# The product of probabilities and v as one float32 product of 64 stationary columns in every batch of a fused attention and MoE kernel

## The chip, the cores and the metric

The kernel runs on one core of one Trainium2 chip, as one program. The metric is the device time of one execution in microseconds (us); lower is better. The core has TensorE (PE; its weight loads are shown as PEld), VectorE (DVE), ScalarE (ACT), GpSimd (POOL) and SyncE (SP), whose queue issues the DMAs here.

## The reference

Three stages follow one another, all in float32: block-causal attention over 4 batches of 8 heads (576 positions, head size 64, blocks of 64), a dense layer with the maximum of three products, and a layer of 4 experts. The change touches the last line of the attention alone.

```python
scores = scale * np.matmul(q, k.transpose(0, 1, 3, 2))     # (4, 8, 576, 64) each
scores = np.where(mask, scores, -1000000000.0)              # block_i >= block_j, blocks of 64
attn = np.exp(scores - np.max(scores, axis=-1, keepdims=True))
attn = attn / (np.sum(attn, axis=-1, keepdims=True) + 1e-09)
attn_out = np.matmul(attn, v)                               # the product of this change
...
h = np.maximum(np.maximum(x @ w1, x @ w2), x @ w3)          # first layer, 2304 tokens
x = h @ w_out
...
out += p[:, e:e + 1] * (np.maximum(x @ w1[e], 0.0) @ w2[e]) # second layer, 4 experts
```

## The kernel before

**Stages.** Heads are numbered g = 0 to 31, eight to a batch, two to a pair. Batch 0 of the attention runs by itself (up to some 103 us). From then on the attention of batch b is mixed with the first layer of batch b - 1: a `Filler` object puts products of `moe1` (the tiles `m`, line 509) between the steps of a head, up to a due count worked out from the head number. The first layer of batch 3 follows alone from 476 us, then the second layer to the end. During batch 1 the weights of the first layer are also converted and split (class `Convert`, lines 432 to 457, on ACT, DVE and POOL) and stored for the later batches.

**Order.** The code issues its steps in a list per head: transposes of probabilities (`ta`, `tb`), scores of the head after next (`s0`, `s1`), values (`va`, `vb`). A scheduler of the framework then orders the instructions of each engine before the program runs; on the chip each engine works its list off in that order.

**Steps of a head that matter here.** `scores` (line 249, tile `st`) makes the scores, DVE finds the extremes (line 263, `mn`), ACT the exponentials (line 270, `p`), POOL multiplies by the reciprocal sums (line 281). `turn_probs` transposes the probabilities by 128 x 128 pieces (line 313, tile `tt` in PSUM) and copies them to SBUF in banks of at most 512 columns. `values` multiplies them with v into the PSUM tiles `pv`, and the result goes to `xf` in SBUF.

**Two ways of that product.** In batch 0 (`g < H`, `values32`) the transposed probabilities stay float32 (`eh`) and v is the raw tile `vraw`, 64 columns as stationary operand: 10 products per head of 128, 384, 384, 128, 256 and five times 64 moving columns, into the lower half of the PSUM partitions; each float32 product becomes two instructions on PE. One ACT copy per part brings the result to `xf` (line 352). In batches 1 to 3 both operands are split into a rounded high part and the rest, as float32r: ACT makes `eh` (line 318) and DVE makes `el` (line 319); POOL makes `vs`, whose 128 columns hold the high part of v beside the low part (lines 161 to 167). The same 10 products are then made twice, with `eh` and with `el` (lines 365 and 373), each one instruction of 128 stationary columns. The two halves of the PSUM partitions are added by an ACT copy to `tmp` and a DVE addition to `xf` (lines 384 and 385).

**Buffers.** `eh` and `el` have one buffer for each part; `pv` comes from its own two PSUM banks in batch 0 and from the four banks shared with `st`, `tt` and `tq` later on.

Of the kernel before, what the change touches and what calls it, by code (L numbers as in the profile page):

```python
# [6 lines left out]
F32 = mybir.dt.float32  # L7
F32R = mybir.dt.float32r
# [17 lines left out]
def program(tc, q, k, v, w1, w2, w3, w_out, probs, e_w1, e_w2, out):  # L26
# [14 lines left out]
    def f(ap):  # L41
        return ap.bitcast(F32)
# [82 lines left out]
    def prep_pair(g):  # L125


        vraw = pairs[g]["vraw"]
        if g < NPAIR and g % 2:

            spare = mp.tile([P, 2 * QW + 2 * S], F32R, name="spare", tag="hh")
            q1, q2 = spare[:, 0:QW], spare[:, QW:2 * QW]
            kk = spare[:, 2 * QW:].rearrange("x (h s) -> x h s", h=2)
        else:
            q1, q2 = (ap_.tile([P, QW], F32R, name=x, tag=x, bufs=1)[:] for x in ("q1", "q2"))
            kk = ap_.tile([P, 2, S], F32R, name="kk", tag="kk", bufs=1)[:]
        nc.gpsimd.memset(q1[:, QT + 64:QT + 128].bitcast(U32), 0)
        q_main = q1[:, 0:QT].rearrange("x (h r p) -> x r h p", h=2, p=64)
        q_tail = q1[:, QT:QW].rearrange("x (t p) -> x t p", p=64)[:, 0:3:2].unsqueeze(1)
        k_all = kk.rearrange("x h (r p) -> x r h p", r=R)  # L140

        def to(n, a, z, step=1):

            if n:
                return k_all[:, a:z:step]
            return q_tail if a == R - 1 else q_main[:, a:z:step]

        turn = turn_parts if g < SPLIT else turn_raw
        turn(g, to, 0)
        if g == 0:  # L150
            nc.scalar.copy(q2[lo], q1[hi])
            nc.vector.tensor_copy(q2[hi], q1[lo])
        else:
            nc.sync.dma_start(out=f(q2[lo]), in_=f(q1[hi]))
            nc.sync.dma_start(out=f(q2[hi]), in_=f(q1[lo]))
        yield
        turn(g, to, 1)
        pairs[g].update(q1=q1, q2=q2, kk=kk)
        if g < NPAIR:
            return  # L160
        vs = ap_.tile([P, 2, 5, P], F32R, name="vs", tag="vs", bufs=2)
        nc.gpsimd.memset(vs[lo, :, 4, :].bitcast(U32), 0)
        for pp, js in ((both, slice(0, 4)), (hi, slice(4, 5))):
            vh = vs[pp, :, js, 0:64]
            rounded(nc.gpsimd, vh, vraw[pp, :, js])
            nc.gpsimd.tensor_tensor(vs[pp, :, js, 64:128], vraw[pp, :, js], f(vh), op=ALU.subtract)
        pairs[g]["vs"] = vs

    def turn_parts(g, to, half):

# [127 lines left out]
    def turn_probs(g, part):  # L298

        hd = heads[g]  # L300
        banks = PARTS[part]
        w = (1024, 256, 640)[part]
        eh = ap_.tile([P, w], F32 if g < H else F32R, name="eh", tag=f"eh{part}", bufs=1)
        el = None if g < H else ap_.tile([P, w], F32R, name="el", tag=f"el{part}", bufs=1)
        (pairs[g // 2] if part == 2 else hd)["e", part] = (eh, el)
        pt = hd["p"] + [pairs[g // 2]["p4"]]
        for n in banks:
            o = 512 * (n - banks[0])
            tt = ps_x.tile([P, 512], F32, name="tt", tag="x")
            c = 0  # L310
            for j, i in BANKS[n]:
                k0 = S - P if j == 4 else j * P
                nc.tensor.transpose(tt[:, c:c + P], pt[i][:, k0:k0 + P], ident)  # L313
                c += P
            if g < H:
                (nc.scalar.copy if n else nc.vector.tensor_copy)(eh[:, o:o + c], tt[:, 0:c])
                continue
            nc.scalar.copy(eh[:, o:o + c], tt[:, 0:c])
            nc.vector.tensor_tensor(el[:, o:o + c], tt[:, 0:c], f(eh[:, o:o + c]), op=ALU.subtract)
        if part == 1 and g % 2 == 0:  # L320
            turn_probs(g, 2)

# [8 lines left out]
            todo += [(j, slice(384, 448), 2, slice(j * P + h * 64, j * P + h * 64 + 64)) for j in range(5)]  # L331
        return todo

    def values32(g, part):

        hd, vraw, h = heads[g], pairs[g // 2]["vraw"], g % 2
        if part == 0:
            hd["pv"] = [ps_v.tile([P, 512], F32, name=f"pv{i}", tag="v") for i in range(2)]
            et = hd["e", 0][0]
            nc.tensor.matmul(out=hd["pv"][0][lo, 0:P], lhsT=vraw[:, h, 0], rhs=et[:, 0:P], start=True, stop=True)  # L340
        for n, (j, to, which, of) in enumerate(products(g, part)):
            et = (pairs[g // 2] if which == 2 else hd)["e", which][0]
            rows = hi if j == 4 else both
            nc.tensor.matmul(  # L344
                out=hd["pv"][1][lo, to], lhsT=vraw[rows, h, j], rhs=et[rows, of],
                start=part == 0 and n == 0, stop=j == 4,
            )
        if part == 0 and h == 0:
            pairs[g // 2]["xf"] = mp.tile([P, S], F32, name="xf", tag="xf", bufs=4)
        xf = pairs[g // 2]["xf"]  # L350
        qs = (slice(0, P), slice(P, S))[part]
        nc.scalar.copy(xf[lo if h == 0 else hi, qs], hd["pv"][part][lo, 0:qs.stop - qs.start])
        if part:
            del heads[g]

    def values(g, part):
        if g < H:
            values32(g, part)
            return
        hd, vs, h = heads[g], pairs[g // 2]["vs"], g % 2  # L360
        if part == 0:

            hd["pv"] = [ps_x.tile([P, 512], F32, name=f"pv{i}", tag="x") for i in range(2)]
            for n, et in enumerate(hd["e", 0]):
                nc.tensor.matmul(
                    out=hd["pv"][0][:, 0:P], lhsT=vs[:, h, 0], rhs=et[:, 0:P], start=n == 0, stop=n == 1
                )
        pv = hd["pv"][1]
        todo = products(g, part)
        for n in range(2):  # L370
            for m, (j, to, which, of) in enumerate(todo):
                et = (pairs[g // 2] if which == 2 else hd)["e", which][n]
                nc.tensor.matmul(  # L373
                    out=pv[:, to], lhsT=vs[:, h, j], rhs=et[:, of],
                    start=part == 0 and n == 0 and m == 0, stop=part == 1 and n == 1 and j == 4,
                )
        if part == 0 and h == 0:
            pairs[g // 2]["xf"] = mp.tile([P, S], F32, name="xf", tag="xf", bufs=4)
        xf = pairs[g // 2]["xf"]
        own, other = (lo, hi) if h == 0 else (hi, lo)  # L380
        qs = (slice(0, P), slice(P, S))[part]
        src = hd["pv"][part][:, 0:qs.stop - qs.start]
        tmp = ap_.tile([P, S - P], F32, name="tmp", tag="tmp", bufs=1)[own, 0:qs.stop - qs.start]
        nc.scalar.copy(tmp, src[other])
        nc.vector.tensor_tensor(xf[own, qs], src[own], tmp, op=ALU.add)
        if part == 0:
            return
        del heads[g]


    tiles = []
# [545 lines left out]
```

## Time and profile before

| | us |
|---|---|
| median of 3 runs | 1335.26 |
| lowest and highest run | 1331.67, 1337.66 |
| the profiled execution, device time | 1333.35 |
| its span, first to last instruction | 1331.6 |

| stretch of the profiled execution | us | PE busy | DVE busy | what runs |
|---|---|---|---|---|
| batch 0 | 0 to 103 | 87.30 | 69.05 | attention alone |
| batches 1 to 3 | 103 to 476 | 366.05 | 262.75 | attention, and first layer of the batch before |
| first layer of batch 3 | 476 to 600 | 115.93 | 57.10 | no attention |
| second layer | 600 to 1331 | 721.00 | 529.49 | experts |

Busy time of PE counts an instruction from its start to its modelled end, and those overlap, so a PE that is busy all the time is read by how many instructions start in a stretch, and by the time from the start of one row to the start of the next.

### The profile page before, as it was taken

How to read it: one execution, taken by the hardware profiler on the slowest of the kernel's cores; microseconds unless marked ns; L12 is line 12 of the kernel's file. 1: busy time of each engine (PE TensorE's matmuls, PEld its weight loads, DVE VectorE, ACT ScalarE, POOL GpSimd, SP SyncE). 2: the span in 40 equal slices, each digit the busy share in tenths (PEclk: the TensorE clock that was granted, in tenths of full speed). 3: DMA queues.
4: the chain of work that ended last, by engine and by line, in shares of the span. 5: the costliest groups of instructions: out<-in, count | busy, mean ns of one | idle time of the engine just before them, and what ended most of it. 6: DMA issues, size and time to landing. Idle time of an engine off the chain costs nothing.

```text
span 1331.6 us, 20943 instructions
## 1 busy us (share of the span) xinstructions
PE 1290.3 (97%) x7670; PEld 1189.9 (89%) x7670; DVE 918.4 (69%) x1685; ACT 542.0 (41%) x1219; POOL 628.7 (47%) x639
## 2 busy tenths in 40 slices
PE   7899989999999989989999999999999999999998
PEld 6569989999999989989999997999999889999997
DVE  6858999665656561178777679677777877777753
ACT  5666656544544430144333343333333433333330
POOL 4856777333334332265444456444454644444420
PEclk9889999999999989999999999999999999999999
DMA  8845677555433344232222222222222133222211
GB/s 200 223 114 137 211 222 213 162 153 145 140 120 117 111 154 147 86 96 88 64 64 79 64 64 87 88 64 64 64 72 78 50 114 91 71 64 64 64 32 48
DMA packets 146983, 142.86 MB, mean 107 GB/s; under 512 B 64576, under 2 KB 112704, under 8 KB 146880
## 3 DMA queue, kind: packets, MB, share of 16 engines
q1 hardware_dynamic: 146880, 141.52, 36.0%
q8 instruction: 60, 0.98, 0.3%
q14 instruction: 43, 0.35, 0.1%
HBM read 114.86 MB, written 17.30 MB: 99 GB/s over the span
## 4 chain that ended last, share of the span: by engine, by line
PE 85%; DVE 9%; issue 2%; DMA 1%; POOL 1%; ACT 1%; SPq 1%; ACTq 0%; POOLq 0%; DVEq 0%
PE m L793 24%; PE m L509 20%; PE o L855 9%; PE o L854 9%; PE o L853 9%; PE st L249 4%; PE pv L373 3%; PE tt L313 3%; PE pv L344 1%; PE tq L175 1%; DVE wt L456 1%; DVE t L715 1%; DVE hl L818 1%; PE tq L194 1%; DMA arena<-in_q 1%
## 5 line engine op out<-in xcount | busy, mean ns | idle before, releaser
L509 PE MATMUL m<-xh,wt 128*128 128x288 f32 x1152 | 259.5, 303 | 1.5 <-DVE mt L547 1.5
L853 PE MATMUL o<-w2h,hh 128*128 128x512 f32 x576 | 224.8, 391 | 4.9 <-DVE arena L860 4.9
L855 PE MATMUL o<-w2h,hl 128*128 128x512 f32 x576 | 225.1, 391 | 0.9 <-DVE hl L818 0.9
L854 PE MATMUL o<-w2l,hh 128*128 128x512 f32 x576 | 224.7, 390 | 0.0
L509 PEld LDWEIGHTS m<-xh,wt 128*128 128x128 f32 x1152 | 193.4, 190 | 2.8 <-DVE mt L547 2.1
L818 DVE SCALAR_TENSOR_TENSOR hl<-c,hh 128x384 fp32r<-128x384 f32 x144 | 166.9, 1179 | 34.1 <-ACT hh L817 33.8
L686 POOL TENSOR_TENSOR w2l<-r,w2h 128x512 fp32r<-128x512 f32 x96 | 130.3, 1378 | 88.1 <-ACT w2h L685 88.0
L509 PE MATMUL m<-xl,wt 128*128 128x288 f32 x576 | 171.5, 298 | 0.0
L686 POOL TENSOR_TENSOR sl<-s,sh 128x1024 fp32r<-128x1024 f32 x48 | 117.4, 2446 | 78.4 <-ACT sh L685 78.4
L686 POOL TENSOR_TENSOR al<-r,ah 128x512 fp32r<-128x512 f32 x48 | 64.4, 1342 | 175.0 <-ACT ah L685 172.0
L860 DVE SCALAR_TENSOR_TENSOR arena<-o,pr,arena 128x512 f32<-128x512 f32 x126 | 93.7, 744 | 71.4 <-PE o L855 71.4
L853 PEld LDWEIGHTS o<-w2h,hh 128*128 128x128 f32 x576 | 108.2, 188 | 23.6 <-DVE arena L860 6.0
L855 PEld LDWEIGHTS o<-w2h,hl 128*128 128x128 f32 x576 | 108.3, 188 | 22.1 <-DVE hl L818 1.6
L817 ACT ACTIVATE hh<-c 128x384 fp32r<-128x384 f32 x144 | 71.2, 519 | 133.2 <-DVE c L812 133.2
L854 PEld LDWEIGHTS o<-w2l,hh 128*128 128x128 f32 x576 | 108.5, 188 | 17.8
L281 POOL TENSOR_SCALAR p<-p,sm 128x128 f32<-128x128 f32 (+2 forms) x144 | 86.4, 617 | 55.1 <-ACT p L270 27.5
L509 PEld LDWEIGHTS m<-xl,wt 128*128 128x128 f32 x576 | 109.5, 190 | 0.6
L270 ACT ACTIVATE p<-st,mn 128x128 f32<-128x128 f32 (+3 forms) x144 | 78.7, 554 | 52.3 <-DVE mn L263 52.0
L685 ACT CAST ah<-r 128x512 fp32r<-128x512 f32 x48 | 29.8, 621 | 156.8 <-issue 117.8
L547 DVE TENSOR_TENSOR mt<-m,mt 128x288 f32<-128x288 f32 x96 | 43.6, 454 | 70.6 <-PE m L509 68.3
L509 PE MATMUL m<-hh,wo 128*128 128x288 f32 x384 | 84.5, 301 | 0.4 <-ACT arena L558 0.4
L549 POOL TENSOR_SCALAR hh<-mt 128x288 fp32r<-128x288 f32 x48 | 23.2, 483 | 125.9 <-DVE mt L547 120.7
(166 smaller groups left out, 3047.2 us busy)
## 6 DMA issues: line engine op xcount, KB each, us to landing
wt<-held SPq DMA_DIRECT2D x54, 512.0 KB, 4.0
r<-in_moe_w SPq DMA_DIRECT2D x48, 512.0 KB, 3.7
r<-in_moe_w SPq DMA_DIRECT2D x96, 256.0 KB, 2.6
arena<-in_moe_w SPq DMA_DIRECT2D x18, 512.0 KB, 4.8
held<-wt SPq DMA_DIRECT2D x18, 512.0 KB, 3.5
wo<-held SPq DMA_DIRECT2D x12, 768.0 KB, 4.3
q<-q SPq DMA_DIRECT2D x26, 304.0 KB, 4.3
arena<-in_q SPq DMA_DIRECT2D x32, 144.0 KB, 3.2
```

What stands on the lines that cost most here:

```text
L249: nc.tensor.matmul(out=st[:, o + c:o + c + n], lhsT=pair[part][:, q0:q0 + P], rhs=pair["kk"][:, x, c:c + n], start=m == 0, stop=m == len(t ...
L270: nc.scalar.activation(x, st[:, o:o + w], ACTF.Exp, bias=mn[:, col:col + 1], scale=-1.0, accum_out=sm[:, col:col + 1],)
L281: nc.gpsimd.tensor_scalar(x, x, sm[:, col:col + 1], 1.0, op0=ALU.mult, op1=ALU.mult)
L509: nc.tensor.matmul(out=out_, lhsT=w, rhs=x, start=m == 0, stop=m == n - 1)
L686: (low or nc.gpsimd).tensor_tensor(dst_l, raw, f(dst_h), op=ALU.subtract)
L793: nc.tensor.matmul(out=m, lhsT=w, rhs=x, start=start and n == 0, stop=stop and n == 3 * KH - 1, skip_group_check=True,)
L817: nc.scalar.activation(h, src, ACTF.Relu)
L818: nc.vector.scalar_tensor_tensor(l, src, 0.0, f(h), op0=ALU.max, op1=ALU.subtract)
L853: nc.tensor.matmul(out=o, lhsT=hh[:, ts], rhs=wh, start=i == 0, stop=False)
L854: nc.tensor.matmul(out=o, lhsT=hh[:, ts], rhs=wl, start=False, stop=False)
L855: nc.tensor.matmul(out=o, lhsT=hl[:, ts], rhs=wh, start=False, stop=i == G - 1)
L860: nc.vector.scalar_tensor_tensor(acc, ov, pr[:, tt, e:e + 1], acc, op0=ALU.mult, op1=ALU.add)
```

## The change

In batches 1 to 3 the product is made as in batch 0: v raw in float32, the transposed probabilities copied once as float32. The split of both operands goes: POOL's `vs` (memset, rounding, subtraction), DVE's `el`, and the second half of the products. So does the addition of the two halves: `xf` is one ACT copy again. The copy of the first bank of each head, which ACT made as `eh`, is now made by DVE (the line that batch 0 had). The tile of transposed probabilities is called `et` and has two buffers for each part in place of one `eh` and one `el`. `pv` stays in the shared PSUM banks from batch 1 on. Function `values32` becomes `values`, with a choice of the PSUM pool.

```diff
     def prep_pair(g):
...
-        if g < NPAIR:
-            return
-        vs = ap_.tile([P, 2, 5, P], F32R, name="vs", tag="vs", bufs=2)
-        nc.gpsimd.memset(vs[lo, :, 4, :].bitcast(U32), 0)
-        for pp, js in ((both, slice(0, 4)), (hi, slice(4, 5))):
-            vh = vs[pp, :, js, 0:64]
-            rounded(nc.gpsimd, vh, vraw[pp, :, js])
-            nc.gpsimd.tensor_tensor(vs[pp, :, js, 64:128], vraw[pp, :, js], f(vh), op=ALU.subtract)
-        pairs[g]["vs"] = vs
...
     def turn_probs(g, part):
...
-        eh = ap_.tile([P, w], F32 if g < H else F32R, name="eh", tag=f"eh{part}", bufs=1)
-        el = None if g < H else ap_.tile([P, w], F32R, name="el", tag=f"el{part}", bufs=1)
-        (pairs[g // 2] if part == 2 else hd)["e", part] = (eh, el)
+        et = ap_.tile([P, w], F32, name="et", tag=f"et{part}", bufs=2)
+        (pairs[g // 2] if part == 2 else hd)["e", part] = et
...
-            if g < H:
-                (nc.scalar.copy if n else nc.vector.tensor_copy)(eh[:, o:o + c], tt[:, 0:c])
-                continue
-            nc.scalar.copy(eh[:, o:o + c], tt[:, 0:c])
-            nc.vector.tensor_tensor(el[:, o:o + c], tt[:, 0:c], f(eh[:, o:o + c]), op=ALU.subtract)
+            (nc.scalar.copy if n else nc.vector.tensor_copy)(et[:, o:o + c], tt[:, 0:c])
...
-    def values32(g, part):
+    def values(g, part):
...
-            hd["pv"] = [ps_v.tile([P, 512], F32, name=f"pv{i}", tag="v") for i in range(2)]
-            et = hd["e", 0][0]
+            pool, tag = (ps_v, "v") if g < H else (ps_x, "x")
+            hd["pv"] = [pool.tile([P, 512], F32, name=f"pv{i}", tag=tag) for i in range(2)]
+            et = hd["e", 0]
...
-            for n, et in enumerate(hd["e", 0]):
-                nc.tensor.matmul(
-                    out=hd["pv"][0][:, 0:P], lhsT=vs[:, h, 0], rhs=et[:, 0:P], start=n == 0, stop=n == 1
-                )
...
-        for n in range(2):
-            for m, (j, to, which, of) in enumerate(todo):
-                et = (pairs[g // 2] if which == 2 else hd)["e", which][n]
-                nc.tensor.matmul(
-                    out=pv[:, to], lhsT=vs[:, h, j], rhs=et[:, of],
-                    start=part == 0 and n == 0 and m == 0, stop=part == 1 and n == 1 and j == 4,
-                )
...
-        tmp = ap_.tile([P, S - P], F32, name="tmp", tag="tmp", bufs=1)[own, 0:qs.stop - qs.start]
-        nc.scalar.copy(tmp, src[other])
-        nc.vector.tensor_tensor(xf[own, qs], src[own], tmp, op=ALU.add)
```

Line numbers of the changed kernel are smaller by 1 to 48; its products with v are lines 326 and 330, the first layer's products line 461, the scores line 239.

On PE, this is how one head of batch 2 stood in the order before (`m` are products of the first layer, `pv` those with v, `st` the scores; 128x384 is output partitions by moving columns):

```order
L365 MATMUL pv_3600<-eh,vs 128x128
L365 MATMUL pv_3600<-el,vs 128x128
L249 MATMUL st<-kk,q_3401 128x320
...
L373 MATMUL pv_3601<-eh,vs 128x384 x2
L373 MATMUL pv_3601<-eh,vs 128x128
L373 MATMUL pv_3601<-el,vs 128x384 x2
L373 MATMUL pv_3601<-el,vs 128x128
L509 MATMUL m<-xh,wt 128x288
...
L373 MATMUL pv_3601<-el,vs 128x256
L373 MATMUL pv_3601<-el,vs 128x64 x5
```

The same head on PE in the changed program:

```order
L326 MATMUL pv_3345<-et,vraw 64x128
L239 MATMUL st<-kk,q_3174 128x320
...
L330 MATMUL pv_3346<-et,vraw 64x384 x2
L330 MATMUL pv_3346<-et,vraw 64x128
L461 MATMUL m<-xh,wt 128x288 x2
...
L330 MATMUL pv_3346<-et,vraw 64x256
L330 MATMUL pv_3346<-et,vraw 64x64 x5
```

The three places of the head's products among the others are the same; each product stands once, with 64 output partitions. Over batches 1 to 3 the 240 products of 64 stationary columns stand in 73 unbroken runs, each between instructions of 128 stationary columns.

On DVE, a piece of the order in batch 1 before (`el` and `xf` are of the split product, `arena` and `wt` of the weight conversion, `mn` of the scores, `mt` of the first layer):

```order
L319 TENSOR_TENSOR el<-tt,eh 128x512
L259 MEMSET st 64x64
L439 TENSOR_SCALAR arena<-arena 128x512
L319 TENSOR_TENSOR el<-tt,eh 128x128
L441 TENSOR_SCALAR arena<-arena 128x512
L385 TENSOR_TENSOR xf<-pv_1659,tmp 64x128
L442 SCALAR_TENSOR_TENSOR arena<-arena 128x512
L259 MEMSET st 64x64 x3
L263 TENSOR_REDUCE mn<-st 128x1 x3
L385 TENSOR_TENSOR xf<-pv_1660,tmp 64x448
```

And a piece at the same work of batch 1 in the changed program:

```order
L394 SCALAR_TENSOR_TENSOR arena<-arena 128x512
L249 MEMSET st 64x64 x2
L253 TENSOR_REDUCE mn<-st 128x1 x3
L499 TENSOR_TENSOR mt<-m,mt 128x288
L249 MEMSET st 64x64
L253 TENSOR_REDUCE mn<-st 128x1
L408 TENSOR_TENSOR wt<-arena,wt 128x512
L304 COPY et<-tt 128x512
```

The subtractions and additions of the split product are gone from between the conversion's steps; one copy of 512 columns per head has come.

## Rows read from the trace of the kernel before

**Rows 1.** The page: the busy time of each engine with its share of the span and its instructions (two parts of the page, the second line being the granted TensorE clock in 40 equal slices of the span, in tenths).

```profile
PE 1290.3 (97%) x7670; PEld 1189.9 (89%) x7670; DVE 918.4 (69%) x1685; ACT 542.0 (41%) x1219; POOL 628.7 (47%) x639
...
PEclk9889999999999989999999999999999999999999
```

**Rows 2.** The table of stretches, batches 1 to 3 of attention: stretch in us, its length, then busy us and (in brackets) the number of instructions of PE, PE weight loads, DVE, ACT and POOL, the granted TensorE clock, the DMA share and GB/s.

```profile
103.00:118.00 15.00, 15.00 (x120) 14.91 (x118) 11.19 (x30) 9.42 (x26) 2.88 (x4) 1.00 0.46 122
118.00:190.00 72.00, 65.39 (x488) 62.79 (x486) 69.38 (x163) 43.52 (x109) 57.20 (x74) 1.00 0.65 200
190.00:200.00 10.00, 9.66 (x64) 9.67 (x65) 9.74 (x26) 7.06 (x20) 7.38 (x14) 0.83 0.97 265
200.00:460.00 260.00, 260.00 (x2007) 258.56 (x2005) 166.67 (x455) 130.48 (x355) 106.97 (x178) 1.00 0.50 145
```

**Rows 3.** The chain of waits within 118 to 190 us, its shares by line (the longest line is cut by the view itself), and the longest wait of PE from 118 to 200 us (us in total, times, longest).

```profile
by line: issue 13.2%; DVE wt L456 11.8%; DVE el L319 9.0%; DVE arena L442 7.8%; DVE mn L263 7.5%; DVE arena L439 6.4%; DVE arena L441 6.2%; DVE mt L547 5.6%; DMA arena<-in_moe_w 4.5%; DVE xf L385 3.8%; POOL arena L446 3.5%; DVE q L213 3.5%;
...
PE tq L194 <- ACT p L270: 2.0, 1, 2.0
```

**Rows 4.** The instructions of line 365, the first product of each head from batch 1 on: min/median/max ns, first and last start in us, shape. One such product stands for each of the 24 heads.

```profile
L365 PE MATMUL pv<-eh,vs x24: 219/223/327, 108.6 to 467.9; 128*128 128x128 f32 x24
```

**Rows 5.** PE in order of time in batch 2: start us, us, then the instruction; rows of one kind are merged, with the shape of the first. First six score products in a row; then the products with v of one head, in its three pieces, and what follows each.

```profile
242.50 1.20 PE L249 MATMUL st<-kk,q 128*128 128x128 f32 x6
243.53 0.29 PE L509 MATMUL m<-hh,wo 128*128 128x288 f32 x1
...
267.69 0.22 PE L365 MATMUL pv<-eh,vs 128*128 128x128 f32 x1
...
267.87 0.36 PE L249 MATMUL st<-kk,q 128*128 128x320 f32 x1
...
268.86 0.57 PE L373 MATMUL pv<-eh,vs 128*128 128x384 f32 x3
269.27 0.62 PE L373 MATMUL pv<-el,vs 128*128 128x384 f32 x3
269.73 0.34 PE L509 MATMUL m<-xh,wt 128*128 128x288 f32 x1
269.92 0.30 PE L509 MATMUL m<-xl,wt 128*128 128x288 f32 x1
270.05 0.43 PE L509 MATMUL m<-xh,wt 128*128 128x288 f32 x2
...
270.58 0.76 PE L373 MATMUL pv<-eh,vs 128*128 128x256 f32 x6
271.17 0.84 PE L373 MATMUL pv<-el,vs 128*128 128x256 f32 x6
271.85 0.38 PE L509 MATMUL m<-xh,wt 128*128 128x288 f32 x1
```

**Rows 6.** PE in order of time at the end of batch 0, the float32 products of two heads in the same three pieces (each product is two instructions, so x12 is one product of 256 columns and five of 64); same columns as Rows 5.

```profile
88.70 0.43 PE L340 MATMUL pv<-eh,vraw 128*64 128x128 f32 x2
89.07 0.33 PE L313 MATMUL tt<-ident,p 128*128 128x128 f32 x1
89.33 1.72 PE L344 MATMUL pv<-eh,vraw 128*64 128x384 f32 x6
90.98 0.84 PE L249 MATMUL st<-kk,q 128*128 128x128 f32 x4
91.75 0.65 PE L344 MATMUL pv<-eh,vraw 128*64 128x256 f32 x2
92.33 0.73 PE L249 MATMUL st<-kk,q 128*128 128x512 f32 x2
92.99 0.93 PE L344 MATMUL pv<-eh,vraw 128*64 128x64 f32 x10
...
101.14 1.36 PE L344 MATMUL pv<-eh,vraw 128*64 128x256 f32 x12
102.43 0.44 PE L175 MATMUL tq<-idents,parts 128*128 128x128 f32 x2
```

**Rows 7.** Weight loads of PE at the same place, in order of time, in the middle of the run of 384-column float32 products.

```profile
90.03 0.14 PEld L344 LDWEIGHTS pv<-eh,vraw 128*64 128x64 f32 x1 [0.18 <-issue]
90.35 0.14 PEld L344 LDWEIGHTS pv<-eh,vraw 128*64 128x64 f32 x1 [0.19 <-issue]
```

**Rows 8.** DVE instructions by line: the two of the split in 118 to 190 us, and the copy of batch 0 in 20 to 103 us (busy us, mean ns of one | idle before).

```profile
L319 DVE TENSOR_TENSOR el<-tt,eh 128x512 fp32r<-128x512 f32 (+2 forms) x18 | 10.1, 572 | 0.1
L385 DVE TENSOR_TENSOR xf<-pv,tmp 64x128 f32<-64x128 f32 (+1 forms) x8 | 3.6, 452 | 0.4 <-ACT tmp L384 0.2
...
L316 DVE COPY eh<-tt 128x512 f32<-128x512 f32 x8 | 5.5, 683 | 2.0 <-PE tt L313 2.0
```

**Rows 9.** Batch 0: three POOL steps on the chain of waits (start us, us), the wait of PE behind them, and the stretch after that in the table of stretches (columns as in Rows 2).

```profile
64.18 0.67 POOL vs L82
...
66.55 1.26 POOL vs L166
...
67.98 0.46 POOL vs L166
...
73.13 0.50 PE L249 MATMUL st<-spare 128*128 128x256 f32 x2 [1.71 <-ACT eh L316]
...
74.00:84.00 10.00, 10.00 (x48) 7.73 (x46) 4.54 (x18) 5.84 (x19) 8.51 (x11) 0.66 0.44 116
```

More of the change, by code (lines that the diff above doesn't have):

```diff
@@ L125, in prep_pair @@
     def prep_pair(g):
-        vraw = pairs[g]["vraw"]
         if g < NPAIR and g % 2:
@@ L332, in products @@
         return todo
-    def values32(g, part):
+    def values(g, part):
         hd, vraw, h = heads[g], pairs[g // 2]["vraw"], g % 2
         if part == 0:
-            hd["pv"] = [ps_v.tile([P, 512], F32, name=f"pv{i}", tag="v") for i in range(2)]
-            et = hd["e", 0][0]
+            pool, tag = (ps_v, "v") if g < H else (ps_x, "x")
+            hd["pv"] = [pool.tile([P, 512], F32, name=f"pv{i}", tag=tag) for i in range(2)]
+            et = hd["e", 0]
             nc.tensor.matmul(out=hd["pv"][0][lo, 0:P], lhsT=vraw[:, h, 0], rhs=et[:, 0:P], start=True, stop=True)
         for n, (j, to, which, of) in enumerate(products(g, part)):
-            et = (pairs[g // 2] if which == 2 else hd)["e", which][0]
+            et = (pairs[g // 2] if which == 2 else hd)["e", which]
             rows = hi if j == 4 else both
@@ L354, in values32 @@
             del heads[g]
[L356 to L363, printed above, removed]
-            for n, et in enumerate(hd["e", 0]):
-                nc.tensor.matmul(
-                    out=hd["pv"][0][:, 0:P], lhsT=vs[:, h, 0], rhs=et[:, 0:P], start=n == 0, stop=n == 1
-                )
-        pv = hd["pv"][1]
-        todo = products(g, part)
-        for n in range(2):
-            for m, (j, to, which, of) in enumerate(todo):
-                et = (pairs[g // 2] if which == 2 else hd)["e", which][n]
-                nc.tensor.matmul(
-                    out=pv[:, to], lhsT=vs[:, h, j], rhs=et[:, of],
-                    start=part == 0 and n == 0 and m == 0, stop=part == 1 and n == 1 and j == 4,
-                )
[L377 to L382, printed above, removed]
-        tmp = ap_.tile([P, S - P], F32, name="tmp", tag="tmp", bufs=1)[own, 0:qs.stop - qs.start]
-        nc.scalar.copy(tmp, src[other])
-        nc.vector.tensor_tensor(xf[own, qs], src[own], tmp, op=ALU.add)
-        if part == 0:
-            return
-        del heads[g]
     tiles = []
```

## The prediction

> **What bounds the kernel now.** I read the page first: PE is busy 97% of the span at nearly full clock [rows 1], so an instruction that PE does not need elsewhere is worth time, and work taken off other engines is worth time only where PE waits for it. The question is therefore asked by stretch [rows 2]. From 200 to 460 us PE is busy all of the 260 us and starts 2007 instructions, 0.1295 us each, while DVE is busy 167 us and POOL 107 us: PE is the bound and nobody else matters. From 118 to 190 us it is otherwise: PE starts only 488 instructions in 72 us, which at 0.1295 us would need 63.2 us, and DVE is busy 69.4 of the 72. The chain of waits in this stretch runs mostly through DVE, with `wt`, `el`, `arena` and `mn` as its largest parts, and the longest wait of PE ends with an exponential that itself came late [rows 3]. This is batch 1, where the weights are converted. So the change gives relief where DVE is the bound, for some 70 us, and is paid on PE everywhere. The 24 heads with the split product start their first product between 108.6 and 467.9 us [rows 4], one per 15.6 us (359.3 over 23).
>
> **PE, per head, before.** The split product of one head stands in three pieces [rows 5]: 0.18 us (267.69 to 267.87) for the two products of 128 columns, 0.87 us (268.86 to 269.73) for the six of 384, 384 and 128, and 1.27 us (270.58 to 271.85) for the twelve of 256 and 64. Together 2.32 us. The first `m` after a piece starts its successor after 0.19 us instead of 0.13 (269.73, 269.92, 270.05); 0.06 for each of the two pieces that `m` follows makes 2.44 us.
>
> **PE, per head, after.** The order shows the same 10 products in the same three pieces, so batch 0 prices them [rows 6]: 0.37 us for the 128-column product (88.70 to 89.07), 1.65 us for 384, 384, 128 (89.33 to 90.98), 1.29 us for 256 and five of 64 (101.14 to 102.43). Together 3.31 us. The neighbours pay too. The six score products that stood in a row took 1.03 us in batch 2 (242.50 to 243.53) [rows 5]; in batch 0 the same six, cut by a product of 64 stationary columns and followed by another, took 0.77 and 0.66 us, 1.43 together (90.98 to 91.75, 92.33 to 92.99) [rows 6]. That is 0.40 us for two such changes there and back, 0.20 each, on instructions that are not v's. Three pieces a head (the order has 73 runs for 24 heads) make 0.60 us, and a head costs 3.91 us. The difference is 1.47 us a head.
>
> What of this is the switch and what the product? Inside a run, float32 instructions of 384 columns start 0.32 us apart [rows 7], two per product; 128 columns are a third of that, 0.11. So the second piece alone would be 4 x 0.32 + 2 x 0.11 = 1.50, not 1.65, and the first 0.22, not 0.37: 0.15 us in each piece is entering and leaving. Without any switch a head costs 3.31 - 0.45 = 2.86 us, 0.42 more than before. The wide products lose (1.50 for 0.87), the third piece gains (1.14 for 1.27). The bounds of this term are thus 0.42 us (switches free between `m` products, which no row of before shows) and 1.47 us (as among scores and transposes in batch 0). I take 1.47, because the scores, like `m`, are float32r products of 128 stationary columns.
>
> The Trainium skill, "TensorEngine Tiling (Array Packing)", section Key Properties, says that a change of tiling mode drains TensorE; that rule speaks against this change, and the trace agrees with 0.35 us a visit (0.15 and 0.20), in batch 0. Its page "FP8 and Floating Point Precision", section TensorE Precision Notes, gives true float32 four passes through the array; an estimate by that page alone, with 1600 moving columns a head at 2.4 GHz, would be 2.67 us for four passes against 1.33 for twice one pass, 1.33 us more a head and 32 us over 24 heads with no switch counted; the rows give 0.42 without a switch, since the old products of 64 columns did not run at their column count.
>
> **PE, by stretch.** 72 us hold 4.6 heads and the 10 us after them 0.6, so 18.7 heads lie where PE has no slack: 18.7 x 1.47 = **+27.5 us**. In 118 to 190 us PE's demand rises to 63.2 + 4.6 x 1.47 = 70.0 us. DVE's falls: `el` 10.1 us and `xf` 3.6 us go [rows 8], the copies that come are 4.6 x 0.683 = 3.1 us, so 69.4 becomes 58.8. The bound moves to PE, and the stretch can end anywhere from 70.0 (no stall left) to 78.8 us (every stall stays). I take 72, so **0**, with bounds -2.0 and +6.8: most stalls stood behind DVE's queue, but the conversion still passes from ACT to DVE to POOL, and some will stay. From 190 to 200 us the clock was granted at 0.83 after the last stall [rows 2]; 64 instructions need 8.3 us, 0.6 head more 0.9: **-0.8** if that drop goes with the stall, +0.9 if not.
>
> **POOL in batch 0.** `vs` of the first pairs of batch 1 is made there, and 0.67 + 1.26 + 0.46 = 2.4 us of it lie on the chain, ahead of a conversion step; behind them PE waits 1.71 us at 73.13, and the next 10 us have a granted clock of 0.66 [rows 9], the lower level of the two (1.2 of 2.4 GHz) for 0.34 / 0.5 of them, some 3.4 us lost. Gone are at most 2.4 + 3.4 = 5.8 us, at least nothing, if the exponentials' scaling and the conversion on the same queue fill the place. I take **-2**, the wait and a little.
>
> **Edits costed at nothing.** ACT loses 24 of its copies to DVE and keeps the others; it is busy half of the time after 200 us [rows 2] and PE does not wait for it there. The extra buffers of `et` and the earlier release of `tt` banks remove no wait that PE shows after 200 us. The addition to `xf` after the last head saves under 0.5 us (0.452 for one, [rows 8]) once. If the cover were gone, that is if PE were not full there, these would be gains, not losses. No DMA is moved.
>
> **Sum.** 27.5 + 0 - 0.8 - 2 = +24.7 us on the profiled execution's 1333.35: **1358 us**. The median of the three runs is 1335.26, 0.14% above that execution, so the basis is the same to within the spread of the runs.
>
> **Rivals.** *The switch is free between first-layer products.* PE then pays 0.42 us a head: 18.7 x 0.42 = 7.9, the batch 1 stretch ends by its demand of 63.2 + 1.9 = 65.1 us or by the chain; with -2 there (part of the stalls stay), -0.8 and -2 the sum is +3, 1336 us, no slower than before by what can be told. With every stall gone (-6.9) and 5.8 in batch 0 it would be 1328. For it: weights are loaded well ahead in a dense stream of `m`. Against: all neighbours in batch 0, float32r ones too, show the switch. It decides when the visit costs under some 0.1 us in place of 0.35. 7%, for same, and 3% for faster. *The stalls of batch 1 stay*, since conversion, not `el`, sets the pace: +6.8 and +0.9 in place of 0 and -0.8, nothing from batch 0: 35.2, 1368 us. For it: `wt`, `arena` lines and POOL's part lead the chain [rows 3]. Against: DVE's queue is what they stand in. 18%. *The change does not do what it says*, with products of batches 1 to 3 still split: the order shows 240 of them with 64 output partitions, so none.
>
> **How the numbers follow.** The forecast has 72%, between 1344 and 1366; what differs inside it is how much of the switch is paid. The range is 1343 to 1368: its lower end is 18.7 heads at 0.95 us (half the switches), 17.8, with -2.0, -0.8 and -5.8 taken, +9.2; its upper end is the second rival. It leaves out the first rival and a little at each end, nearly 2 in 10. A measurement of this kernel can tell about 0.5% (6.7 us) from no change; so slower 0.9, same 0.07, faster 0.03.
>
> **What would show it.** In the changed profile: PE full from 200 us to the end of attention, with DVE far from it; float32 instructions of 384 columns 0.32 us apart; a gap about 0.1 us longer on entering and on leaving a run of `pv`, and the first `m` after it late; attention of batch 3 ending some 25 us later; the stages after it unchanged in length. Wrong would be: `m` around `pv` at its usual 0.13 us (first rival), or a PE that still waits 7 us or more between 118 and 200 us (second).

## The result and the profile after

The changed kernel took 1352.42 us, the median of 4 runs (1351.42 to 1352.73); the kernel before, on the same chips, 1333.76. The ratio is 1.0135, with a 95% interval of 1.0109 to 1.0162: slower by some 18.7 us. The forecast was 1358 in a range of 1343 to 1368. The profiled executions are 1352.73 against 1333.35 us, spans 1350.5 against 1331.6, so the ledger below has 18.9 us to account for.

The page of the changed kernel, as in [rows 1]:

```profile
PE 1317.9 (98%) x7670; PEld 1175.3 (87%) x7670; DVE 860.6 (64%) x1565; ACT 528.8 (39%) x1195; POOL 588.1 (44%) x579
...
PEclk9899999999999999999999999999999999999999
```

The same number of PE instructions, busy 27.6 us longer; every other engine has less to do. The table of stretches, to be read against [rows 2] and the last row of [rows 9] (stretch, length, busy us and instructions of PE, weight loads, DVE, ACT, POOL, granted clock, DMA share, GB/s):

```profile
74.00:84.00 10.00, 10.00 (x70) 7.69 (x71) 6.73 (x22) 7.54 (x23) 8.71 (x12) 1.00 0.38 117
118.00:190.00 72.00, 71.29 (x504) 62.63 (x502) 63.15 (x149) 45.09 (x116) 51.34 (x68) 1.00 0.70 213
190.00:200.00 10.00, 9.55 (x73) 8.44 (x71) 9.53 (x20) 4.94 (x13) 5.82 (x9) 1.00 1.05 281
200.00:460.00 260.00, 260.00 (x1834) 230.21 (x1834) 116.16 (x350) 113.59 (x319) 74.11 (x127) 1.00 0.49 136
```

From 200 to 460 us PE is still busy all the time and starts 1834 instructions where it started 2007; DVE fell from 167 to 116 us there, and nothing came of it. From 118 to 190 us PE is nearly full (71.3 of 72 us) and starts 504 instructions where it started 488. The granted clock is 1.00 from 74 to 84 us, where it was 0.66, and from 190 to 200 us, where it was 0.83.

PE in order of time around the products of one head of batch 2, to be read against [rows 5] and [rows 6]:

```profile
268.06 0.29 PE L461 MATMUL m<-xh,wt 128*128 128x288 f32 x1
268.28 0.43 PE L326 MATMUL pv<-et,vraw 128*64 128x128 f32 x2
268.64 0.71 PE L239 MATMUL st<-kk,q 128*128 128x320 f32 x3
269.19 0.29 PE L461 MATMUL m<-xh,wt 128*128 128x288 f32 x1
269.32 0.29 PE L461 MATMUL m<-xl,wt 128*128 128x288 f32 x1
269.54 1.72 PE L330 MATMUL pv<-et,vraw 128*64 128x384 f32 x6
271.19 0.53 PE L461 MATMUL m<-xh,wt 128*128 128x288 f32 x2
271.56 0.29 PE L461 MATMUL m<-xl,wt 128*128 128x288 f32 x1
...
272.49 0.29 PE L461 MATMUL m<-xh,wt 128*128 128x288 f32 x1
272.72 1.36 PE L330 MATMUL pv<-et,vraw 128*64 128x256 f32 x12
274.01 0.40 PE L461 MATMUL m<-xh,wt 128*128 128x288 f32 x1
274.25 0.30 PE L461 MATMUL m<-xl,wt 128*128 128x288 f32 x1
```

The three pieces take 0.36, 1.65 and 1.29 us, 3.30 together. The `m` before a piece takes 0.22 or 0.23 us instead of 0.13; the first `m` after one 0.24 (274.01 to 274.25), and the two from 271.19 take 0.37 where two take 0.26. That is 0.09 before, 0.15 inside a piece as in batch 0, 0.10 after: 0.34 us a visit (a visit is one run of 64-column products between 128-column ones).

The x12 of the third piece holds two shapes. Its products of 64 moving columns by themselves, in narrower windows (the first two instructions, of 256 columns, are left out):

```profile
273.20 0.63 PE L330 MATMUL pv<-et,vraw 128*64 128x64 f32 x8
273.76 0.32 PE L330 MATMUL pv<-et,vraw 64*64 64x64 f32 x2
```

The last key block has only 64 rows, so the last product (two instructions) uses 64 rows and 64 columns. The eight before it start 0.06 us apart (0.41 us from the first start to the last, in the trace); the first 64-row instruction starts 0.15 us after the last of them. The third piece thus pays for a change of rows too: its products alone would take some 1.01 us (2 x 0.216 + 10 x 0.058, starts in the trace), its 1.29 less the 0.15 of the visit are 1.14, so some 0.13 go with the change of rows.

The head starts give the ledger. Head 8 started at 108.62 us before and head 31 at 467.9 [rows 4]; head 14 before, and heads 8, 14 and 31 after, from PE in order of time:

```profile
205.66 0.22 PE L365 MATMUL pv<-eh,vs 128*128 128x128 f32 x1
```

```profile
103.74 0.43 PE L326 MATMUL pv<-et,vraw 128*64 128x128 f32 x2
```

```profile
199.60 0.43 PE L326 MATMUL pv<-et,vraw 128*64 128x128 f32 x2
```

```profile
487.74 0.43 PE L326 MATMUL pv<-et,vraw 128*64 128x128 f32 x2
```

| part | before, us | after, us | difference | as predicted |
|---|---|---|---|---|
| start to head 8 | 108.6 | 103.7 | -4.9 | -2 |
| head 8 to head 14 | 97.0 | 95.9 | -1.2 | some +0.6 |
| head 14 to head 31 | 262.3 | 288.1 | +25.9 | 17 x 1.47 = +25.0 |
| head 31 to the end | 863.7 | 862.8 | -0.9 | +1.1 |

(The last column spreads the prediction's terms over the same parts: the 0.6 is 0.9 for the 0.6 heads between 108.6 and 118 us, -0.8 for 190 to 200 us, and 0.5 for what lies between 200 and 205.7.)

The ledger is of one execution of each kernel. From head 14 to head 31 it repeats: 288.1 us again in the two versions of the changed kernel below that have the same order (one buffer; the split of v put back). Ahead of head 8 it does not: the changed kernel and the six versions below that have its order through batch 0 start head 8 anywhere from 103.0 to 107.2 us, and the kernel before alone spreads from 1330.4 to 1339.6 us in 23 executions. A microsecond or two in the first two rows is no finding.

### The profile page after: what moved, and what is told of

It reads as the page before. It is cut to its first block, busy times and chain, and to the rows that moved or that the text cites. A ratio compares the mean times of both kernels' runs of the same rounds, so it can differ in the third digit from the quotient of the medians.

```text
span 1350.5 us, 20728 instructions
## 1 busy us (share of the span) xinstructions
PE 1317.9 (98%) x7670; PEld 1175.3 (87%) x7670; DVE 860.6 (64%) x1565; ACT 528.8 (39%) x1195; POOL 588.1 (44%) x579
## 4 chain that ended last, share of the span: by engine, by line
PE 88%; DVE 6%; issue 2%; POOL 1%; DMA 1%; ACT 1%; SPq 0%; ACTq 0%; POOLq 0%; DVEq 0%
PE m L745 24%; PE m L461 22%; PE o L807 9%; PE o L806 9%; PE o L805 9%; PE pv L330 6%; PE st L239 4%; PE tt L302 3%; PE pv L326 1%; DVE hl L770 1%; PE tq L184 1%; DMA r<-in_moe_w 1%; PE tq L165 1%; DVE t L667 1%; DMA q<-q 0%
## 5 line engine op out<-in xcount | busy, mean ns | idle before, releaser
L330 PE MATMUL pv<-et,vraw 128*64 128x64 f32 (+4 forms) x576 | 104.6, 315 | 0.0
```

Source lines behind the costliest of these rows:

```text
L330: nc.tensor.matmul(out=hd["pv"][1][lo, to], lhsT=vraw[rows, h, j], rhs=et[rows, of], start=part == 0 and n == 0, stop=j == 4,)
```

## The experiments

The times are medians, with the ratio to the kernel before as run on the same chip; the kernel before itself was 1334.9 us beside the first four runs, 1335.6 beside the second four and 1336.5 beside the last three.

**128 stationary columns.** Is it the float32 product that costs, or the change between 64 and 128 stationary columns?

```diff
-        vraw = ap_.tile([P, 2, 5, D], F32, name="vraw", tag="vraw", bufs=4)
+        vraw = ap_.tile([P, 5, 2, D], F32, name="vraw", tag="vraw", bufs=4)
+        nc.gpsimd.memset(vraw[lo, 4], 0.0)
...
-                out=hd["pv"][1][lo, to], lhsT=vraw[rows, h, j], rhs=et[rows, of],
+                out=hd["pv"][1][:, to], lhsT=vraw[:, j].rearrange("p h d -> p (h d)"), rhs=et[:, of],
```

> The changed kernel, its float32 products made with 128 stationary columns (v of both heads of the pair side by side, one half of the output not used; the rows of the last key block that hold nothing are zero), so that PE never changes between 64 and 128 stationary columns. All results stay those of the reference. Theory (0.34 us for each of three visits to 64 columns): a head costs 2.75 to 3.3 us in place of 3.9, so 24 heads save 15 to 28 us and the eight of batch 0 up to 8 more: 1322 to 1338 us. Rival (the float32 passes are the whole cost, the change of columns is nothing): 1350 to 1358 us, or more, since weight loads of 128 columns take longer.

Measured: 1345.54 us, ratio 1.0077 (1.0051 to 1.0102); some 7 us less than the changed kernel, but above the 1322 to 1338 expected. PE around a head of batch 2 in this kernel:

```profile
259.54 0.30 PE L462 MATMUL m<-xh,wt 128*128 128x288 f32 x1
259.67 0.38 PE L327 MATMUL pv<-et,vraw 128*128 128x128 f32 x2
259.89 2.11 PE L330 MATMUL pv<-et,vraw 128*128 128x384 f32 x8
261.65 0.48 PE L462 MATMUL m<-xh,wt 128*128 128x288 f32 x1
261.97 0.29 PE L462 MATMUL m<-xl,wt 128*128 128x288 f32 x1
...
264.38 0.29 PE L462 MATMUL m<-xh,wt 128*128 128x288 f32 x1
264.51 1.00 PE L330 MATMUL pv<-et,vraw 128*128 128x64 f32 x8
265.32 0.38 PE L462 MATMUL m<-xh,wt 128*128 128x288 f32 x1
265.53 0.29 PE L462 MATMUL m<-xl,wt 128*128 128x288 f32 x1
```

The `m` before a piece takes 0.13 us again (259.54 to 259.67, 264.38 to 264.51), so that surcharge goes with the change of columns. On the `m` after a piece part of it stays: 0.21 us at 265.32, against 0.24 in the changed kernel and 0.19 before [rows 5], so 0.06 to 0.08 of the 0.10 after a visit is not the change of columns. The zero rows also take away the 64-row shape of the last product, so this kernel tests both changes at once. But the products of 64 moving columns now start some 0.1 us apart (8 in 0.81 us), as with float32r before, against 0.06 with 64 stationary columns. From head 14 to head 31 a head takes 16.28 us (205.1 to 481.8), against 16.95 in the changed kernel and 15.43 before: 0.67 us of the 1.5 come back, the low edge of the 0.6 to 1.2 expected. Over the last 18 heads that is 12 us. But head 8 starts at 107.9 us, 4.2 later than in the changed kernel, after a wait of PE for a copy on ACT and 10 us at the lower clock from 73.8 on:

```profile
74.02 0.79 PE L240 MATMUL st<-spare 128*128 128x256 f32 x2 [2.71 <-ACT et L305]
```

Head 14 is 5.5 later (205.1): up to there cheaper products gave nothing. So the change of shape is shown as a cause where PE is full; what was missed is the part before.

**The split from head 14 on.**

```diff
+PLAIN = 14
...
-        if g < NPAIR:
+        if g < PLAIN // 2:
             return
...
-        if g < H:
+        if g < PLAIN:
             values32(g, part)
```

> The kernel before, with the unsplit float32 product for heads 0 to 13 in place of 0 to 7, the split one from head 14 on. Theory (relief where DVE is the bound, loss where PE is): head 14 starts some 6 to 8 us earlier as in the changed kernel, and from there on everything runs at the pace of before: 1325 to 1329 us. Rival (the gain up to head 13 is only work put off, given back when the split begins): 1333 to 1336 us.

Measured: 1329.06 us, ratio 0.995 (0.9933 to 0.9968). Head 14 starts at 199.6 us, as in the changed kernel, 6.1 before the kernel before, and the pace behind it is that of before (PE starts 2006 instructions from 200 to 460 us, before 2007). Nothing is given back. Of the 6.1 us, 5.3 are there when head 8 starts (103.3 against 108.6), so most of the gain lies in batch 0 and little in the six heads of batch 1. This version beats both kernels, by 0.5% over the kernel before.

**Without DVE's low part.**

```diff
-        el = None if g < H else ap_.tile([P, w], F32R, name="el", tag=f"el{part}", bufs=1)
+        el = None if g < H else eh
...
-            nc.vector.tensor_tensor(el[:, o:o + c], tt[:, 0:c], f(eh[:, o:o + c]), op=ALU.subtract)
```

> The kernel before, without DVE's subtraction for the low part of the probabilities: the second half of the products takes the high part again, so the output leaves that correction wrong; PE has the same instructions. Theory (DVE's queue is what holds PE in batch 1): most of PE's some 10 us of stall in 118 to 200 us go, 1324 to 1329 us. Rival (the conversion of the weights on ACT, DVE and POOL sets the pace by itself): 1332 to 1336 us.

Measured: 1334.2 us, ratio 0.9991 (0.9971 to 1.001): no gain, as the rival said, though not quite for its reason. The table of stretches of this run, and PE's wait within it:

```profile
118.00:190.00 72.00, 68.06 (x509) 65.51 (x508) 66.03 (x156) 46.63 (x121) 57.08 (x77) 1.00 0.67 204
200.00:204.00 4.00, 0.88 (x7) 0.45 (x5) 2.25 (x4) 1.77 (x5) 3.84 (x6) 0.83 1.09 300
204.00:208.00 4.00, 3.97 (x16) 4.00 (x17) 1.25 (x2) 0.65 (x2) 1.16 (x2) 0.50 1.01 325
208.00:212.00 4.00, 4.00 (x27) 4.00 (x26) 2.58 (x9) 1.77 (x4) 1.01 (x1) 0.82 1.05 314
```

```profile
204.03 0.61 PE L249 MATMUL st<-kk,q 128*128 128x320 f32 x1 [2.69 <-DMA q<-q]
```

From 118 to 190 us PE starts 509 instructions in place of 488 and DVE has 66.0 us of work in place of 69.4, so the relief is there: head 13 starts at 188.9 us, 4.4 earlier than before. Then PE waits 2.69 us for the transfer that copies one half of `q` to the other partitions, which took 9.4 us on the chain (194.5 to 203.9) while the DMA engines were busy throughout. The lower clock sets in during the wait and holds for 6.8 us (1.4 us of 200 to 204, all of 204 to 208, 1.4 of 208 to 212). Head 14 starts at 207.3, 1.6 later than before. A transfer took the place of DVE in this execution.

**Without the low part and without the split of v.** As the kernel above, and:

```diff
+    vs = ap_.tile([P, 2, 5, P], F32R, name="vs", tag="vs", bufs=1)
+    nc.gpsimd.memset(vs[:].bitcast(U32), 0x3F800000)
...
-        vs = ap_.tile([P, 2, 5, P], F32R, name="vs", tag="vs", bufs=2)
-        nc.gpsimd.memset(vs[lo, :, 4, :].bitcast(U32), 0)
-        for pp, js in ((both, slice(0, 4)), (hi, slice(4, 5))):
...
```

> As the kernel without the low part of the probabilities, and v is not split either: one constant tile of ones stands for the split v, so POOL makes no split of v and the output is not attention's. Theory (POOL's split of v lies on batch 0's chain and its stall lowers the clock): batch 0 is 3 to 5 us shorter, 1320 to 1325 us. Rival (batch 0 of the changed kernel is shorter by its second buffers for the transposed probabilities): no shorter than without the low part alone, 1324 to 1329 us.

Measured: 1328.17 us, ratio 0.9947 (0.993 to 0.9965), the upper end of the rival's range, but not for its reason. Heads 4 and 5 are 9.3 us apart in place of 12.4 before, and the wait at 71 to 73 us is gone with POOL's split of v; but head 8 starts only 0.9 us earlier (107.7), as a wait for the copy of `q`, which ends at 46 to 47 us in both, is longer in this run (4.0 us against 2.6), with 6.8 us at the lower clock from 45.6 us on, which the kernel before does not have there. The other instructions stand in another order too, from some 66 us on. The price in batch 0 stayed open here.

**One buffer for the transposed probabilities.**

```diff
-        et = ap_.tile([P, w], F32, name="et", tag=f"et{part}", bufs=2)
+        et = ap_.tile([P, w], F32, name="et", tag=f"et{part}", bufs=1)
```

> The changed kernel with one buffer in place of two for each part of the transposed probabilities. Theory (the shorter batch 0 and batch 1 come from the work taken off POOL and DVE): no difference that can be told, 1349 to 1356 us. Rival (the second buffer is what shortened batch 0 and took waits out of batch 1): 1356 to 1362 us.

Measured: 1352.39 us, ratio 1.0136 (1.012 to 1.0152), the changed kernel's time. The second buffers do nothing here.

**The split of v put back, unread.**

```diff
         pairs[g].update(q1=q1, q2=q2, kk=kk)
+        if g < NPAIR:
+            return
+        vraw = pairs[g]["vraw"]
+        vs = ap_.tile([P, 2, 5, P], F32R, name="vs", tag="vs", bufs=2)
...
```

> The changed kernel with POOL's split of v put back, its result read by nobody. Theory (POOL's split of v on batch 0's chain, and the clock behind it, cost 3 to 5 us): 1355 to 1358 us. Rival (batch 0 is shorter by the order that the instructions came to stand in, whatever POOL does): 1350 to 1354 us.

Measured: 1354.14 us, ratio 1.015 (1.0131 to 1.0168), between the two expectations. It doesn't tell them apart: with nobody to read it the scheduler placed the split elsewhere. POOL in order of time, first before, then here:

```profile
64.18 0.66 POOL L82 TENSOR_SCALAR vs<-vraw 64x128 fp32r<-64x128 f32 x1
64.92 1.63 POOL L446 TENSOR_TENSOR arena<-arena 128x512 int32<-128x512 int32 x1
66.51 1.30 POOL L166 TENSOR_TENSOR vs<-vraw,vs 128x512 fp32r<-128x512 f32 x1
67.76 0.14 POOL L137 MEMSET q<- 128x64 uint32 x1
67.98 0.46 POOL L166 TENSOR_TENSOR vs<-vraw,vs 64x128 fp32r<-64x128 f32 x1
68.53 1.04 POOL L82 TENSOR_SCALAR wt<-arena 128x512 fp32r<-128x512 f32 x1
69.55 1.26 POOL L446 TENSOR_TENSOR arena<-arena 128x512 int32<-128x512 int32 x1
```

```profile
67.39 0.76 POOL L82 TENSOR_SCALAR wt<-arena 128x512 fp32r<-128x512 f32 x1
68.83 1.29 POOL L407 TENSOR_TENSOR arena<-arena 128x512 int32<-128x512 int32 x1 [0.68 <-DVE arena L403]
70.92 2.72 POOL L280 TENSOR_SCALAR p<-p,sm 128x128 f32<-128x128 f32 x3 [0.80 <-DVE sm L278]
73.62 1.31 POOL L82 TENSOR_SCALAR vs<-vraw 128x512 fp32r<-128x512 f32 x2
75.02 1.67 POOL L166 TENSOR_TENSOR vs<-vraw,vs 128x512 fp32r<-128x512 f32 x1
```

Before, POOL had the split between two conversion steps and worked without a pause until 70.8 us; here the conversion's step of 68.53 comes at 67.39 and the split only at 73.62. Heads 4 and 5 are 8.3 us apart, as in the changed kernel. All other instructions stand in the changed kernel's order here, from the first to the last; with the split of v among them, head 8 to head 14 takes 97.9 us in place of 95.9, and the pace behind that is the same.

**The low part put back, unread.**

```diff
+        el = None if g < H else ap_.tile([P, w], F32, name="el", tag=f"el{part}", bufs=1)
...
+            if g >= H:
+                nc.vector.tensor_tensor(el[:, o:o + c], tt[:, 0:c], et[:, o:o + c], op=ALU.subtract)
```

> The changed kernel with DVE's subtraction for the low part of the probabilities put back in heads 8 to 31, its result read by nobody; PE has the same products. Theory (DVE holds PE in batch 1, and nowhere else): batch 1 gets 3 to 8 us longer, the later batches not: 1355 to 1361 us. Rival (with float32 products PE is the bound in batch 1 too, DVE's 53 us are covered): 1350 to 1354 us.

Measured: 1355.9 us, ratio 1.0159 (1.0143 to 1.0176). The time lies where the theory put it, but not for its reason: the 3.5 us more are already there when head 8 starts (107.2 us against 103.7), in batch 0, which has next to none of this work (the first `el` starts at 102.6 us) and the same order; they are the spread ahead of head 8. From head 8 to head 31 this kernel takes 383.5 us and the changed one 384.0, from head 8 to head 14 96.7 and 95.9. Where PE has the float32 products, 53 us of DVE are covered but for some 0.8 us in batch 1. The rival is right on that.

**Mixed columns.** The kernel with the split from head 14 on, and 128 stationary columns in heads 8 to 13 (the layout of v changes with it, and POOL clears the empty rows):

```diff
-                out=hd["pv"][1][lo, to], lhsT=vraw[rows, h, j], rhs=et[rows, of],
+                out=hd["pv"][1][lo if g < H else both, to],
+                lhsT=vraw[rows, j, h] if g < H else vraw[:, j].rearrange("p h d -> p (h d)"), rhs=et[rows, of],
```

> The kernel with unsplit float32 products up to head 13 and split ones from head 14, and the products of heads 8 to 13 with 128 stationary columns (v of both heads side by side). Theory (0.67 us a head of switching and rows, where PE is the bound): up to 4 us less than with 64 columns there, 1324 to 1328 us. Rival (in batch 1 PE is not the bound once the split is gone, so cheaper products give nothing): 1328 to 1331 us.

Measured: 1330.88 us, ratio 0.9961 (0.9949 to 0.9974): no gain over 64 columns there, as the rival said. From head 8 to head 14 it takes 100.6 us (104.9 to 205.5) against 96.2, with PE busy 68.1 of the 72 us from 118 to 190 us against 71.3 with 64 columns: PE has less to do there and waits more.

**Without the split of v alone.** Diff as for the kernel without both, with `el` kept.

> The kernel before, with a constant tile of ones for the split v, so POOL makes no split of v and the output is not attention's; the low part of the probabilities and all products stay. Theory (POOL's split of v, where it stood in the order before, delays a conversion step, behind which ACT's copy for PE is queued at 71 to 73 us, and the clock falls after that wait): heads 4 to 5 are 8 to 9.5 us apart in place of 12.5, the time 1329 to 1332 us. Rival (that wait comes from the order on ACT alone, and stays): 12 us or more, 1333 to 1336 us.

Measured: 1326.43 us, ratio 0.9929 (0.9902 to 0.9955), 9 to 10 us less than before and better than expected. Its table of stretches:

```profile
74.00:84.00 10.00, 9.26 (x47) 6.53 (x47) 5.79 (x17) 5.56 (x19) 8.41 (x11) 0.83 0.90 214
118.00:190.00 72.00, 70.85 (x533) 68.61 (x532) 70.35 (x177) 47.61 (x122) 51.61 (x69) 1.00 0.68 208
```

Heads 4 and 5 are 10.2 us apart, less than the 12.4 of before and more than expected, and head 8 starts 1.1 us earlier only. The larger part comes in batch 1: PE starts 533 instructions from 118 to 190 us in place of 488, with DVE as busy as before (70.4 us) and POOL at 51.6 in place of 57.2. Head 8 to head 14 takes 90.4 us in place of 97.0. Up to head 13, which no late transfer touches yet, the gain from head 8 on is 7.0 us without the split of v, 4.4 without `el` and 7.1 without both. So taking either away relieves the same stalls, and POOL's split of v counts for more than DVE's `el`. How much of it is the work itself isn't shown: without the split of v the other instructions stand in another order from some 66 us on, without `el` from some 106 us on.

**The split from head 20 on, and from head 12 on** (`PLAIN = 20`, `PLAIN = 12`).

> Unsplit float32 products up to head 19, split ones from head 20 on. Theory (1.5 us a head from head 14 on, where PE is full): 6 heads more than with the step at head 14, 1336 to 1340 us. Rival (the loss of the changed kernel comes later, where it has more products of the first layer's second half beside it): 1329 to 1333 us.

Measured: 1336.51 us, ratio 1.0007 (0.9993 to 1.0021). Head 14 to head 20 takes 103.1 us (201.3 to 304.4), against 93.9 with the step at head 14 (199.6 to 293.5): 1.53 us a head.

> Unsplit float32 products up to head 11, split ones from head 12 on. Theory (from 104 to 200 us the length is set by the conversion of the weights and PE has room, so a head costs the same there either way): the same as with the step at head 14, 1327 to 1332 us. Rival (each head more in float32 there is a gain, by DVE's relief): 1331 to 1335 us.

Measured: 1326.46 us, ratio 0.993 (0.9902 to 0.9958); head 14 starts at 198.2 us against 199.6. Its stretch from 118 to 190 us, then that of the kernel with the step at head 20 from 200 us:

```profile
118.00:190.00 72.00, 71.35 (x523) 65.66 (x522) 64.99 (x160) 46.20 (x118) 50.68 (x66) 1.00 0.74 220
```

```profile
200.00:460.00 260.00, 260.00 (x1936) 247.31 (x1937) 147.58 (x412) 124.01 (x343) 97.69 (x165) 1.00 0.50 143
```

With the step at head 12 PE starts 523 instructions from 118 to 190 us, and the time is a little under that with the step at head 14 (1329.06; ratios 0.9902 to 0.9958 and 0.9933 to 0.9968, which overlap), just below the range expected. The float32 product is not a gain in itself there; it is free. With the step at head 20 PE starts 1936 instructions from 200 us on, between 1834 and 2007. This step at head 12 is the best of the versions that compute the whole.

## Why the prediction held, and where it missed

**PE per head: right.** Expected 3.31 us in the pieces and 0.60 on the neighbours, found 3.30 and some 0.58; expected 1.47 us a head more, found 1.52 from head 14 to head 31 (25.9 over 17), and 1.53 in the kernel with the step at head 20. The choice of 1.47 rather than 0.42, which rested on the scores of batch 0 standing for `m`, is what the result hangs on, and rows and experiment bear it out: `m` pays 0.09 before and 0.10 after each visit, and with 128 stationary columns nothing before and 0.06 to 0.08 after. The Trainium skill, "TensorEngine Tiling (Array Packing)", section Key Properties, says that changing the tiling mode drains TensorE; the trace agrees, with 0.34 us a visit beside float32r products too, most of it the change of columns. The first rival falls. One working was off without moving the sum: the third piece was put at 1.14 us without a switch, but it holds the change to 64 rows as well, so its products alone are some 1.01, a head without any switch 2.73 rather than 2.86, and the lower bound 0.29 rather than 0.42.

**Batch 1: the size held, the reason only in part.** The term for 118 to 190 us was 0, and from head 8 to head 14 the changed kernel takes 1.2 us less. PE is busy 71.3 of the 72 us there, but that the bound moved to its products isn't shown: cheaper products gave nothing in the two kernels with 128 stationary columns (97.3 and 100.6 us from head 8 to head 14, against 95.9 and 96.2 with 64), though both also have POOL clear rows of v and stand in another order. So that the term came out near 0 is partly luck. The prediction put most of the stalls of before on DVE's queue. Taking 10 us off DVE alone gave 4.4 us, and a late transfer took them back; putting 53 us back on DVE in the changed kernel cost some 0.8 us; taking only the split of v off POOL gave 6.6 us from head 8 to head 14, with DVE as busy as before. This fits stalls of the weight conversion, which passes through ACT, DVE and POOL, with more weight on POOL than the prediction gave it; but the order of the instructions changed in these kernels as well, so the shares stay open.

**POOL in batch 0: the step that was mis-sized.** The term was -2 us of at most 5.8, and head 8 starts 4.9 us earlier. The wait of 1.71 us at 73.13 [rows 9] is not there, and the clock from 74 to 84 us is 1.00. From head 4 to head 8 the gain is 6.4 us (34.3 in place of 40.7), and start to head 4 is 1.5 us longer, which is within the spread. The prediction's mechanism, POOL's split ahead of a conversion step, is supported by the two kernels without the split, in which heads 4 and 5 move from 12.4 to 9.3 and 10.2 us apart. But it is not the whole: from head 4 to head 8 these two gain only 2.3 us (without the split alone) and 3.9, in another order of the instructions; and the changed kernel with 128 stationary columns has no split of v either, yet PE waits 2.71 us there for the same copy on ACT, and its heads 4 and 5 are 16.7 us apart. How much of the rest is the order that the instructions came to stand in isn't settled, since unread work doesn't go back to its old place. The extra buffers are excluded.

**The second rival** (stalls stay, 1368 us) falls: PE waits about 1 us from 103 to 200 us (0.7 and 0.4, its only two waits there).

**After the last head** the changed kernel is 0.9 us faster where 1.1 slower was implied; before, 6.8 us at the lower clock followed the end of attention (from 488 us), in the changed kernel 3.4 us (from 511). The sum was 24.7 us and came to 18.9 in the profiled spans: of the 5.8 between them, 2.9 are batch 0, 1.8 batch 1 and 2.0 the end, less 0.9 in the 17 heads.

## What to carry to other kernels

Price a matmul of fewer stationary columns by its neighbours: in a stream of 128-column products each run of 64-column ones costs about a third of a microsecond, most of which no instruction's own duration shows, so it pays only where PE has slack; whether longer runs would make it pay no run here shows. A saving on other engines is worth what the stretch's own chain gives, and the busiest engine of a stretch need not be the one that holds PE: take the candidates off one at a time. Where a trade is free in one stage and costs in another, make the choice by stage: the float32 product up to head 11 and the split one behind it beat both whole versions, with most of the gain ahead of head 8. Taking an instruction away also lets the scheduler order the others anew: only where that order stays the same, as with the split of v put back, is a difference the work's own.

## What the runs showed of the hardware that was not expected

A float32 product of 64 moving columns starts every 0.06 us per instruction with 64 stationary columns and every 0.11 us with 128, so narrower weights do help where the moving side is short; on five products a head that is 0.5 us, half of what the three visits cost (an estimate from these rows). And relief on DVE turned into a lower clock: PE reached a transfer 2.69 us too early and stood; the clock fell to 1.2 GHz during the wait, and PE worked some 5.4 us more at that level, which at half the pace is another 2.7 us (an estimate), as much as the wait itself.
